# A chunked scan, a routed layer and a cosine layer in one kernel: the first expert's two token lists are cut at another tile

## The chip, the cores and the metric

The kernel runs on one core of a Trainium2 chip. The metric is the device time of one execution in microseconds (us); lower is better. TensorE (PE) multiplies matrices, VectorE (DVE), ScalarE (ACT) and GpSimd (POOL) work elementwise, and SP issues most of the DMA transfers. Each engine takes its instructions strictly in the order in which the program lists them.

## The reference, cut to what matters

```python
# 1: scan over chunks; 4 x 8 heads, 768 positions, 32 channels -> x: 3072 tokens x 256
y = (C B^T * L) x + (C state) * decay ;  state = decay_full * state + B^T x
# 2: routed layer, E = 8 experts, w1 256 x 1024, w2 1024 x 256
expert_idx = argmax(cos(x, expert_emb) / tau);  gate_w = softmax(...)[expert_idx]
for e in range(E):
    mask = expert_idx == e
    out[mask] = gate_w[mask, None] * (relu(x[mask] @ w1[e]) @ w2[e])
# 3: dense layer, w_in 256 x 2048, w_out 2048 x 256
h = x @ w_in ;  out = (h * cos(h)) @ w_out
```

## The kernel before, in words

The kernel has three stages. The first makes the tokens in 24 tiles of 128 (`for n in range(N)`, L546), finds each token's expert and sends its row into that expert's list in device memory with an indirect DMA (`scatter`, L804; one POOL instruction per tile). The tiles are routed in groups of 4, 4, 4, 4, 4, 2, 1 and 1 (`g.SIZES`, L715); a group's chain of small DVE operations (`group`, L298) hands its rows to `g.done`, from which `finish` scatters them. The second stage runs the experts one after the other (L1238). The third is the dense layer (L1354 on).

All products of the second and third stage are made from operands that are split into a rounded part and a rest (fp32r), with three matmuls for each product: high by high, rest by high, high by rest. The moving operand's width is the number of places in the list: 432 for experts 1 to 7.

Expert 0 is treated apart. Its list is cut in two. The tokens of the first twelve tiles (the groups up to number `g.EARLY = 2`) go to rows 0 to 255 of the buffer, those of the last twelve to rows 2048 to 2303. The first list is worked on by the generator `window` (L925) while the first stage is still running: a load, the gate weights (`gates`, 11 steps and one for each column of rows), transposes, 48 matmuls up, 48 down. The second list is loaded by `second_list` (L978) after the last scatter and takes expert 0's place in the loop at L1238, again with 48 and 48 matmuls.

Where a generator's next step goes in the order of the program is written out by hand: `g.WN` says how many steps of `window` stand behind tile n, and in the strings `g.TAIL` and `g.END` each letter is a step (w: `window`, x: `second_list`, c: the counts, with `fill(1)` and the load of list 1; r: `load_w1(1)`; f: `fill(2)`; k: two matmuls that only keep PE busy; g: gates of list 1; m, l, r, t in TAIL: the last tile's steps). Behind the counts stands a conditional block for lists that overflow (L1144), which every engine passes.

The SP queue behind it holds, in this order: `load_w2(1)` (L752), `rows_of(2)` (the load of list 2, L904), `fill(3)` (L891, zeros behind list 3's end), `load_w1(2)` (L746), the first pieces of the dense layer's weights (`fetch`, L1089) and `load_w2(2)`. The first of these pieces is read by ACT at L1107, in the middle of expert 1's loop.

Of the kernel before, what the change touches and what calls it, by code (L numbers as in the profile page):

```python
# [8 lines left out]
F32 = mybir.dt.float32  # L9
F32R = mybir.dt.float32r  # L10
# [3 lines left out]
AF = mybir.ActivationFunctionType  # L14
ALU = mybir.AluOpType
# [8 lines left out]
RW = 274  # L24
# [23 lines left out]
def attn_router(ctx, tc, g):  # L48

    nc = tc.nc  # L50
# [408 lines left out]
    k = 0  # L459
    while k < len(tiles):  # L460
        n = g.SIZES[len(groups)]
# [84 lines left out]
    for n in range(N):  # L546
        for k in range(max(3, n + g.AHEAD[n]), min(N, n + 1 + g.AHEAD[n + 1])):
            pre(*tiles[k])
        if n >= 3:
            logits_of(n - 3)  # L550
        t, b = tiles[n]
        if n > 1:
            front(t, b)
        if t + 1 < NSTEP:
            if b == 1:
                side = [blocks(t + 1)]
            if b == (1 if t else 3):
                preps[t + 1] = prep(t + 1)
                next(preps[t + 1])
            if b == 2 and t + 2 < NSTEP:  # L560
                load_a(t + 2)
        for s_ in side:
            next(s_, None)
            if b == 3:
                for _ in s_:
                    pass
        if n >= 1:
            t, b = tiles[n - 1]
            if n > 1:
                mid(t, b)  # L570

            if t + 1 < NSTEP:
                late.append((t + 1, b))
            while late and late[0][0] in preps:
                next(preps[late.pop(0)[0]])
            if b == 3 and t + 2 < NSTEP:
                load_b(t + 2)
        if n >= 2:
            if n == 2:
                for _ in constants_:  # L580
                    pass
            rows_of(n - 2)
        for _ in g.done[:2 if n > 12 else 1]:
            finish()
        for _ in range(g.ZN.get(n, 0)):
            next(zeros)
        g.each(n)
        win(g.WN.get(n, 0))
# [60 lines left out]


CAP = 432
CE = 256
S2 = 2048
NL = E + 1
CQ = CAP // 4
# [6 lines left out]
def tile_attention_moe_moe2(ctx: ExitStack, tc: tile.TileContext, A1, A2, X, BNh, BT, CT, cst_d, emb, tau, w1, w2, w_in, w_out, out):  # L662
    nc = tc.nc
    ET = mybir.EngineType
    g = G_()
# [10 lines left out]
    xs = dp.tile([E * SX, RW], F32, name="xs")  # L676
# [11 lines left out]
    g.FIRST = 6  # L688
    g.GE = "vava"
    g.GW = "va"  # L690
    g.EARLY = 2
    g.ZN = {4: 3, 8: 1, 13: 1}
    g.PX = 5
    g.PX0 = 4
# [32 lines left out]
    x0 = il[:, 0]  # L727
# [94 lines left out]
    def quarters(x):  # L822
        return x.rearrange("(p k) d -> p (k d)", k=4)

    def zeros(cst):

        zrow = wA.tile([CQ, 4 * RW], F32, tag="l2", name="zrow")
        nc.gpsimd.memset(zrow, 0.0)
        yield
        for k in (0, S2):  # L830
            nc.gpsimd.dma_start(quarters(xs[k:k + CE, :]), zrow[:CE // 4])
# [5 lines left out]
        nc.vector.memset(capf[:, 0:2], float(CE))  # L837
        yield
        nc.gpsimd.dma_start(quarters(zd), zrow)
        yield  # L840
# [54 lines left out]

    def places(e):

        return (CE // 2, 2) if e == 0 else (CQ, 4)

    def rows_of(e):  # L900
        P, K = places(e)
# [10 lines left out]
    def turned(xg):  # L912
        px = bank("px")
        for k in range(2):
            for m in range(2):
                nc.tensor.transpose(px.rearrange("p (m c k) -> p m c k", m=2, k=2)[:, m, :, k], xg[:, k, 136 * m:136 * m + 128], ident)
        return px

    def parts(px, xh, xl):
        nc.scalar.copy(xh, px)  # L920
        yield
        nc.vector.tensor_tensor(out=xl, in0=px, in1=xh.bitcast(F32), op=ALU.subtract)
        return [x.rearrange("p (m c) -> p m c", m=2) for x in (xh, xl)]

    def window():  # L925

        xg = xp.tile([128, 4, RW], F32, tag="xg", name="xg", bufs=2)[:, :2]
        i = nc.sync.dma_start(xg, xs[:CE, :].rearrange("(p k) d -> p k d", k=2))
        early.append(i.ins)
        yield  # L930
        yield from gates(xg, g.sb2, g.GW, -1)
        w = {k: W[0][k].rearrange("p (a b) -> p a b", a=2) for k in ("h1", "l1")}

        px = turned(xg)
        yield
        x_ = g.apool.tile([128, 1024], F32R, tag="XB0", name="x_")
        xh, xl = yield from parts(px, *(x_[:, 512 * k:512 * k + 512] for k in range(2)))
# [4 lines left out]
        hl = g.sb2.tile([128, 2048], F32R, tag="ac", name="hl")  # L942
        lo = split_lo(0, "2", g.L2)
        py = g.psY.tile([128, 2, 512], F32, tag="y", name="py")[:, :, :CE]

        def down(q):
            l2 = W[0]["l2"].rearrange("p (a b) -> p a b", a=8)
            for f in (2 * q, 2 * q + 1):
                s = slice(CE * f, CE * f + CE)
                for m in range(2):  # L950
                    for k, (a_, b_) in enumerate(((w["h2"], hh), (w["h2"], hl), (l2, hh))):
                        nc.tensor.matmul(py[:, m], lhsT=a_[:, f, 128 * m:128 * m + 128], rhs=b_[:, s], start=f == 0 and k == 0, stop=f == 7 and k == 2)
# [24 lines left out]

    def second_list():  # L978

        xg = g.xg0 = rows_of(0)  # L980
        for j in fills:
            tc.declare_no_dep(loads[0], j, reason="the first list lies before the others")
        yield
        yield from gates(xg, g.sb2, g.GW)
        yield
        px = turned(xg)
        yield
        g.x0 = yield from parts(px, *(x0[:, 512 * k:512 * k + 512] for k in range(2)))
        yield

    g.window = window()
# [58 lines left out]
    nc.scalar.copy(yd[:, :, :CE], g.y0)  # L1050
    g.pctx.close()

    with ExitStack() as mctx:
# [426 lines left out]
```

## Time and profile before

| | us |
|---|---|
| median of three runs (576.4 to 576.64) | 576.6 |
| the profiled execution, its own time | 577.55 |
| span of the profiled execution, first to last instruction | 575.9 |

The span lies 1.65 us inside the profiled execution's own time, which lies 0.95 us above the median. Times within the trace count from the start of the span. The first stage reaches to about 123 us, the experts to 297.6 us, the dense layer to the end. A matmul's bar in the trace is longer than the distance to the next one, because they overlap; the price of a matmul in a run of equal ones is that distance.

### The profile page before, as it was taken

What the parts mean: (1) busy time and instruction counts of PE and PEld (TensorE: products, weight loads), DVE (VectorE), ACT (ScalarE), POOL (GpSimd) and SP (SyncE); (2) the same over time, 40 slices, a digit from 0 to 9 for tenths busy, and PEclk for the clock granted to TensorE, in tenths of its full rate; (3) what the DMA queues carried; (4) which work ended last, traced back from release to release, by engine and by line L of the source; (5) the groups of instructions that cost most, each with busy time, mean ns of one, the idle gap of its engine ahead of it and who ended that gap; (6) DMA issues with size and microseconds to landing.
All of it is one profiled execution on the core that took longest, in us unless ns stands there. A gap on an engine that the chain in (4) does not pass through costs nothing.

```text
span 575.9 us, 10962 instructions
## 1 busy us (share of the span) xinstructions
PE 550.4 (96%) x3964; PEld 498.8 (87%) x3964; DVE 438.6 (76%) x861; ACT 294.0 (51%) x629; POOL 315.0 (55%) x348
## 2 busy tenths in 40 slices
PE   8898999989889999989999999999999999999995
PEld 4786887888879999979988999999999999999994
DVE  5997999766497798888849877766677777776882
ACT  4433444435465567656646545446445445445562
POOL 4635452452274476455636646646646745755763
PEclk9899899989989999989999999999999999999998
DMA  6999884138766655653210000000100100100000
GB/s 195 224 241 200 208 227 153 40 113 233 250 197 192 214 150 194 236 200 119 78 2 1 2 1 9 28 1 2 37 1 1 38 0 2 38 0 9 31 20 19
DMA packets 28777, 56.26 MB, mean 98 GB/s; under 512 B 7232, under 2 KB 16080, under 8 KB 28096
## 3 DMA queue, kind: packets, MB, share of 16 engines
q1 hardware_dynamic: 26032, 47.03, 28.9%
q0 software_dynamic: 2688, 8.50, 4.3%
q8 instruction: 32, 0.52, 0.4%
q14 instruction: 25, 0.20, 0.1%
HBM read 47.76 MB, written 11.07 MB: 102 GB/s over the span
## 4 chain that ended last, share of the span: by engine, by line
PE 56%; DVE 8%; issue 3%; ACT 3%; DMA 2%; POOL 1%; SPq 1%; POOLq 0%; ACTq 0%; DVEq 0%
PE po L1399 22%; PE pu L1365 22%; PE py L1224 6%; PE ph L1256 5%; DVE hl L1261 2%; DVE ta L1109 1%; POOL gl L1436 1%; DMA xg<-xs 1%; DVE ta L1111 1%; ACT hh L1260 1%; DMA r<-in_w 1%; DVE xl L1078 1%; DVE lg L861 1%; ACT h L760 1%; DVE ta L1115 1%
## 5 line engine op out<-in xcount | busy, mean ns | idle before, releaser
L1436 POOL TENSOR_TENSOR gl<-gg,gh 128x512 fp32r<-128x512 f32 (+1 forms) x111 | 125.8, 1138 | 105.1 <-PE pu L1365 63.3
L1426 ACT ACTIVATE cc<-ff,half 128x512 f32<-128x512 f32 (+1 forms) x112 | 74.2, 663 | 129.2 <-DVE ff L1424 121.6
L1422 DVE TENSOR_SCALAR tt<-pu 128x512 f32<-128x512 f32 (+1 forms) x110 | 67.4, 613 | 64.9 <-PE pu L1365 61.5
L1399 PE MATMUL po<-h,gl 128*128 128x256 f32 x384 | 108.3, 282 | 0.0
L1399 PE MATMUL po<-l,gh 128*128 128x256 f32 x384 | 108.2, 282 | 0.0
L1399 PE MATMUL po<-h,gh 128*128 128x256 f32 x382 | 107.7, 282 | 0.0
L769 POOL TENSOR_TENSOR l<-r,h 128x512 fp32r<-128x512 f32 x50 | 67.8, 1371 | 59.5 <-ACT h L760 55.7
L1399 PEld LDWEIGHTS po<-h,gh 128*128 128x128 f32 x382 | 72.3, 189 | 3.6
L1399 PEld LDWEIGHTS po<-l,gh 128*128 128x128 f32 x384 | 72.6, 189 | 3.1
L1399 PEld LDWEIGHTS po<-h,gl 128*128 128x128 f32 x384 | 73.1, 190 | 0.1
L1424 DVE SCALAR_TENSOR_TENSOR ff<-tt,pu 128x512 f32<-128x512 f32 (+1 forms) x110 | 67.0, 609 | 3.8
L1365 PE MATMUL pu<-yh,il 128*128 128x512 f32 (+1 forms) x192 | 68.6, 357 | 0.0
L1365 PE MATMUL pu<-yh,ih 128*128 128x512 f32 (+1 forms) x192 | 68.3, 356 | 0.0
L1365 PE MATMUL pu<-yl,ih 128*128 128x512 f32 (+1 forms) x192 | 68.0, 354 | 0.0
L1432 DVE SCALAR_TENSOR_TENSOR gg<-pu,cc 128x512 f32<-128x512 f32 (+1 forms) x110 | 66.6, 605 | 0.4 <-ACT cc L1426 0.4
L1435 ACT CAST gh<-gg 128x512 fp32r<-128x512 f32 (+1 forms) x112 | 60.8, 543 | 0.4 <-DVE gg L1432 0.3
L1261 DVE SCALAR_TENSOR_TENSOR hl<-ph,hh 128x432 fp32r<-128x432 f32 (+1 forms) x64 | 36.7, 576 | 23.4 <-ACT hh L1260 23.2
L1224 PE MATMUL py<-hl,h 128*128 128x432 f32 (+1 forms) x128 | 46.3, 362 | 4.1 <-DVE hl L1261 4.0
L1224 PE MATMUL py<-hh,h 128*128 128x432 f32 (+1 forms) x128 | 45.5, 356 | 1.6 <-ACT hh L1260 1.6
L1224 PE MATMUL py<-hh,l 128*128 128x432 f32 (+1 forms) x128 | 45.5, 356 | 0.0
L1260 ACT ACTIVATE hh<-ph 128x432 fp32r<-128x432 f32 (+1 forms) x64 | 32.8, 512 | 22.5 <-PE ph L1256 21.5
L1256 PE MATMUL ph<-xh,h 128*128 128x432 f32 x112 | 41.2, 368 | 0.0
(228 smaller groups left out, 1199.6 us busy)
## 6 DMA issues: line engine op xcount, KB each, us to landing
r<-in_w SPq DMA_DIRECT2D x32, 512.0 KB
ac<-acd SPq DMA_DIRECT2D x8, 512.0 KB
raw<-in_w_in SPq DMA_DIRECT2D x8, 512.0 KB
raw<-in_w_out SPq DMA_DIRECT2D x8, 512.0 KB
xg<-xs SPq DMA_DIRECT2D x7, 462.4 KB
XB<-in_X SPq DMA_DIRECT2D x10, 256.0 KB
xs<-zd SPq DMA_DIRECT2D x5, 462.4 KB
bt<-in_BT SPq DMA_DIRECT2D x6, 256.0 KB
```

The costliest lines, as they stand in the source:

```text
L769: (nc.vector if engines[q] == "v" else nc.gpsimd).tensor_tensor(out=l[:, s], in0=W[e][rn][:, s], in1=h[:, s].bitcast(F32), op=ALU.subtract)
L1224: nc.tensor.matmul(py[m][:, :b_.shape[1]], lhsT=a_[:, q, 128 * m:128 * m + 128], rhs=b_, start=q == 0 and k == 0, stop=q == 7 and k == 2)
L1256: nc.tensor.matmul(ph[:, :n], lhsT=a_[:, c, 128 * f:128 * f + 128], rhs=b_[:, c], start=k == 0, stop=k == 5)
L1261: nc.vector.scalar_tensor_tensor(out=hl, in0=ph[:, :n], scalar=0.0, in1=hh.bitcast(F32), op0=ALU.max, op1=ALU.subtract)
L1365: nc.tensor.matmul(PU[u], lhsT=a_[:, c, 128 * f:128 * f + 128], rhs=b_[:, c], start=c == 0 and k == 0, stop=c == 1 and k == 2)
L1399: nc.tensor.matmul(po[:, i], lhsT=a_[:, s], rhs=b_, start=first and per == 1, stop=q == NF - 1 and k == 2 and i == per - 1)
L1422: nc.vector.tensor_scalar(tt, pu, 0.25, MAGIC, op0=ALU.add, op1=ALU.add)
L1424: nc.vector.scalar_tensor_tensor(out=ff, in0=tt, scalar=-MAGIC, in1=pu, op0=ALU.add, op1=ALU.subtract)
L1426: nc.scalar.activation(cc, ff, AF.Sin, bias=half, scale=-TWO_PI)
L1432: nc.vector.scalar_tensor_tensor(out=gg, in0=pu, scalar=TWO_PI, in1=cc, op0=ALU.mult, op1=ALU.mult)
L1435: nc.scalar.copy(gh, gg)
L1436: (nc.vector if u >= len(units) else nc.gpsimd).tensor_tensor(out=gl, in0=gg, in1=gh.bitcast(F32), op=ALU.subtract)
```

## The change

Expert 0's lists are cut behind tile 16 instead of tile 12. The first list gets 320 places (80 partitions of four rows), the second 192 (96 partitions of two rows). Both matmul loops keep their 48 and 48 instructions; their width changes. In `window` each 128-row slice f of the hidden layer now has a PSUM bank of its own (eight evacuations of 320 columns in place of four of 512), and the transposes fill two banks. From tile 19 on up to four rows of `g.done` are scattered behind one tile. The steps of `window` begin behind tile 20 instead of 19, and TAIL and END are written anew.

```diff
-        for _ in g.done[:2 if n > 12 else 1]:
+        for _ in g.done[:4 if n > 18 else 2 if n > 12 else 1]:
             finish()
...
-CE = 256
+CE1, CE2 = 320, 192
...
-    g.EARLY = 2
+    g.EARLY = 3
...
-    g.WN = {19: 1, 20: 5, 21: 2, 22: 5}
-    g.TAIL = "tltttwtwtwmrttttttlrttttwltttttwttwttttttttttt"
-    g.END = "wxwcwccwcwwcwwwwwcwxwxwrxxfcxxxwwxxxxgxkkgkkggxxxxxg"
+    g.WN = {20: 1, 21: 7, 22: 7, 23: 1}
+    g.TAIL = "tltttwtwtmrttttttlrttttwltttttwttttwttttttttt"
+    g.END = "wxwwcwcwcwwcwwwwcwwwwwcwwwwrxxfcwxxxwwxwxxxgxkkgkkggxxxxxg"
...
-        xg = xp.tile([128, 4, RW], F32, tag="xg", name="xg", bufs=2)[:, :2]
-        i = nc.sync.dma_start(xg, xs[:CE, :].rearrange("(p k) d -> p k d", k=2))
+        xg = xp.tile([128, 4, RW], F32, tag="xg", name="xg", bufs=2)[:CE1 // 4]
+        i = nc.sync.dma_start(xg, xs[:CE1, :].rearrange("(p k) d -> p k d", k=4))
         early.append(i.ins)
         yield
-        yield from gates(xg, g.sb2, g.GW, -1)
+        yield from gates(xg, g.sb2, 2 * g.GW, -1)
...
-        for q in range(4):
-            ph = bank("ph")
-            for j in range(2):
-                f = 2 * q + j
-                k = 0
-                for c in range(2):
-                    for a_, b_ in ((w["h1"], xh), (w["h1"], xl), (w["l1"], xh)):
-                        nc.tensor.matmul(ph[:, CE * j:CE * j + CE], lhsT=a_[:, c, 128 * f:128 * f + 128], rhs=b_[:, c], start=k == 0, stop=k == 5)
-                        k += 1
-                yield
-            s = slice(512 * q, 512 * q + 512)
-            nc.scalar.activation(hh[:, s], ph, AF.Relu)
-            nc.vector.scalar_tensor_tensor(out=hl[:, s], in0=ph, scalar=0.0, in1=hh[:, s].bitcast(F32), op0=ALU.max, op1=ALU.subtract)
-            yield
-            next(lo)
-            if q >= 2:
-                down(q - 2)
-            yield
-        down(2)
-        yield
-        down(3)
-        yield
+        for f in range(8):
+            ph = bank("ph")[:, :CE1]
+            k = 0
+            for c in range(2):
+                for a_, b_ in ((w["h1"], xh), (w["h1"], xl), (w["l1"], xh)):
+                    nc.tensor.matmul(ph, lhsT=a_[:, c, 128 * f:128 * f + 128], rhs=b_[:, c], start=k == 0, stop=k == 5)
+                    k += 1
+            yield
+            hh, hl = hs[f]
+            nc.scalar.activation(hh, ph, AF.Relu)
+            nc.vector.scalar_tensor_tensor(out=hl, in0=ph, scalar=0.0, in1=hh.bitcast(F32), op0=ALU.max, op1=ALU.subtract)
+            yield
+            if f % 2 == 0:
+                next(lo)
+            if f >= 4:
+                down(f - 4)
+            yield
+        for f in range(4, 8):
+            down(f)
+            yield
...
         def wide(e):
-            return CE if e == 0 else CAP
+            return CE2 if e == 0 else CAP
```

## Rows read from the trace of the kernel before

**Rows 1.** The page: busy time and share of each engine

```profile
PE 550.4 (96%) x3964; PEld 498.8 (87%) x3964; DVE 438.6 (76%) x861; ACT 294.0 (51%) x629; POOL 315.0 (55%) x348
```

**Rows 2.** Stretches: length; busy PE, PEld, DVE, ACT, POOL; granted clock; DMA share; GB/s

```profile
115.00:120.00 5.00, 3.14 (x39) 2.80 (x38) 1.92 (x10) 1.84 (x7) 3.36 (x8) 1.00 0.32 114
120.00:125.00 5.00, 4.73 (x29) 4.56 (x30) 3.68 (x20) 2.58 (x10) 3.18 (x6) 0.69 0.18 59
...
140.00:145.00 5.00, 5.00 (x46) 5.00 (x45) 4.97 (x14) 4.72 (x12) 0.65 (x1) 1.00 0.87 226
...
155.00:160.00 5.00, 3.25 (x14) 2.51 (x14) 2.06 (x5) 3.08 (x7) 1.43 (x2) 0.95 1.05 371
```

**Rows 3.** Chain that ended last: start, length, runs of fp32r matmuls (432, 256, 512 columns)

```profile
284.62 1.18 PE ph L1256 x6
...
310.52 1.43 PE po L1399 x12
311.94 1.39 PE pu L1365 x6
```

**Rows 4.** PE in order of time: plain f32 matmuls under and at 256 columns, transposes

```profile
88.88 0.73 PE L277 MATMUL pt<-IE,yT 128*128 128x136 f32 x4
89.45 1.22 PE L214 MATMUL ps<-CB,BTb 128*128 128x256 f32 x4
...
142.03 0.91 PE L1070 MATMUL px<-ident,xg 108*128 108x108 f32 x8
```

**Rows 5.** Groups by form: PE's transposes, busy and mean ns of one

```profile
L1070 PE MATMUL px<-ident,xg 108*128 108x108 f32 x56 | 6.6, 257 | 0.6 <-DVE xg L884 0.6
```

**Rows 6.** POOL in order of time: scatters of tiles 12, 13, 16, 17, 23; list's power

```profile
100.12 1.22 POOL L805 DMA_INDIRECT xs<-yr,pi  x1 [10.26 <-ACT yr L285]
101.64 0.97 POOL L805 DMA_INDIRECT xs<-yr,pi  x1 [0.21 <-issue]
...
114.15 0.96 POOL L805 DMA_INDIRECT xs<-yr,pi  x1 [7.28 <-ACT xg L886]
115.42 0.97 POOL L805 DMA_INDIRECT xs<-yr,pi  x1 [0.23 <-ACT yT L267]
...
125.26 0.96 POOL L805 DMA_INDIRECT xs<-yr,pi  x1 [0.54 <-issue]
...
131.41 1.22 POOL L857 TENSOR_TENSOR r<-xg,pw 128x2 f32<-128x2 f32 x1 [3.62 <-DMA xg<-xs]
```

**Rows 7.** DVE in order of time: tile 22's product and group 4's sum

```profile
108.27 0.69 DVE L233 TENSOR_TENSOR M<-ps,L 128x512 f32<-128x512 f32 x1 [0.24 <-PE ps L214]
...
110.38 0.16 DVE L339 TENSOR_TENSOR acc<-acc,asum 128x8 bf16<-128x8 bf16 x1
```

**Rows 8.** PE in order of time: group 4's counts, keep-warm matmuls, expert 0's first matmuls

```profile
112.17 0.18 PE L343 MATMUL pc<-oh,tri 128*128 128x32 bf16 x1
...
134.16 1.10 PE L412 MATMUL pw<-warm 128*128 128x272 bf16 x8
...
137.00 0.50 PE L1256 MATMUL ph<-il,h 128*128 128x256 f32 x2 [1.30 <-ACTq L1144]
```

**Rows 9.** ACT in order of time: last tile, first list's result, dense layer's first weights

```profile
119.85 0.37 ACT L267 COPY yT<-py 128x256 f32<-128x256 f32 x1 [2.85 <-remote]
...
136.22 0.59 ACT L1050 COPY yd<-py 128x512 f32<-128x512 f32 x1
...
156.79 0.66 ACT L1107 ACTIVATE tb<-raw 128x512 f32<-128x512 f32 x1 [5.73 <-DMA raw<-in_w_in]
```

**Rows 10.** SP's queue in order of time: second list, `load_w2(1)`, first `fetch`

```profile
127.87 3.33 SPq L904 DMA_DIRECT2D xg<-xs  x2
...
137.72 1.90 SPq L752 DMA_DIRECT2D r<-in_w  x2
...
149.61 0.43 SPq L1089 DMA_DIRECT2D raw<-in_w_in  x1
```

**Rows 11.** Chain that ended last, around 141 us: start, length, what

```profile
141.75 6.06 DMA xg<-xs
```

More of the change, by code (lines that the diff above doesn't have):

```diff
@@ L829, in zeros @@
         yield
-        for k in (0, S2):
-            nc.gpsimd.dma_start(quarters(xs[k:k + CE, :]), zrow[:CE // 4])
+        for k, n in ((0, CE1), (S2, CE2)):
+            nc.gpsimd.dma_start(quarters(xs[k:k + n, :]), zrow[:n // 4])
             yield
@@ L836, in zeros @@
         nc.vector.memset(capf, float(CAP))
-        nc.vector.memset(capf[:, 0:2], float(CE))
+        nc.vector.memset(capf[:, 0:1], float(CE1))
+        nc.vector.memset(capf[:, 1:2], float(CE2))
         yield
@@ L896, in places @@
     def places(e):
-        return (CE // 2, 2) if e == 0 else (CQ, 4)
+        return (CE2 // 2, 2) if e == 0 else (CQ, 4)
     def rows_of(e):
@@ L910, in bank, with turned @@
         return g.psS.tile([128, 2, 4, 64], F32, tag="s", name=nm).rearrange("p a b c -> p (a b c)")
-    def turned(xg):
-        px = bank("px")
-        for k in range(2):
+    def turned(xg, wide=False):
+        P, K = xg.shape[:2]
+        px = [bank("px") for _ in range(1 + wide)]
+        px = [(px[m] if wide else px[0][:, P * K * m:])[:, :P * K] for m in range(2)]
+        for k in range(K):
             for m in range(2):
-                nc.tensor.transpose(px.rearrange("p (m c k) -> p m c k", m=2, k=2)[:, m, :, k], xg[:, k, 136 * m:136 * m + 128], ident)
+                nc.tensor.transpose(px[m].rearrange("p (c k) -> p c k", k=K)[:, :, k], xg[:, k, 136 * m:136 * m + 128], ident[:P, :P])
         return px
     def parts(px, xh, xl):
-        nc.scalar.copy(xh, px)
+        n = px[0].shape[1]
+        for m in range(2):
+            nc.scalar.copy(xh[:, m], px[m])
         yield
-        nc.vector.tensor_tensor(out=xl, in0=px, in1=xh.bitcast(F32), op=ALU.subtract)
-        return [x.rearrange("p (m c) -> p m c", m=2) for x in (xh, xl)]
+        for m in range(2):
+            nc.vector.tensor_tensor(out=xl[:, m], in0=px[m], in1=xh[:, m].bitcast(F32), op=ALU.subtract)
+        return xh, xl
     def window():
-        xg = xp.tile([128, 4, RW], F32, tag="xg", name="xg", bufs=2)[:, :2]
-        i = nc.sync.dma_start(xg, xs[:CE, :].rearrange("(p k) d -> p k d", k=2))
+        xg = xp.tile([128, 4, RW], F32, tag="xg", name="xg", bufs=2)[:CE1 // 4]
+        i = nc.sync.dma_start(xg, xs[:CE1, :].rearrange("(p k) d -> p k d", k=4))
         early.append(i.ins)
         yield
-        yield from gates(xg, g.sb2, g.GW, -1)
+        yield from gates(xg, g.sb2, 2 * g.GW, -1)
         w = {k: W[0][k].rearrange("p (a b) -> p a b", a=2) for k in ("h1", "l1")}
-        px = turned(xg)
+        px = turned(xg, True)
         yield
-        x_ = g.apool.tile([128, 1024], F32R, tag="XB0", name="x_")
-        xh, xl = yield from parts(px, *(x_[:, 512 * k:512 * k + 512] for k in range(2)))
+        x_ = g.apool.tile([128, 2048], F32R, tag="XB0", name="x_")
+        xh, xl = yield from parts(px, *(x_[:, 2 * CE1 * k:2 * CE1 * k + 2 * CE1].rearrange("p (m c) -> p m c", m=2) for k in range(2)))
         yield
@@ L942, in window @@
         hl = g.sb2.tile([128, 2048], F32R, tag="ac", name="hl")
+        he = g.sb2.tile([128, 1024], F32R, tag="BTb", name="he")
+        hs = [[z[:, CE1 * f:CE1 * f + CE1] for z in (hh, hl)] for f in range(6)]
+        hs += [[z[:, CE1 * f:CE1 * f + CE1] for z, f in ((x_, 4 + f), (he, f))] for f in range(2)]
         lo = split_lo(0, "2", g.L2)
-        py = g.psY.tile([128, 2, 512], F32, tag="y", name="py")[:, :, :CE]
-        def down(q):
+        py = g.psY.tile([128, 2, 512], F32, tag="y", name="py")[:, :, :CE1]
@@ L947, in down @@
+        def down(f):
             l2 = W[0]["l2"].rearrange("p (a b) -> p a b", a=8)
[L948 to L952, printed above, removed]
-        for q in range(4):
-            ph = bank("ph")
-            for j in range(2):
-                f = 2 * q + j
-                k = 0
-                for c in range(2):
-                    for a_, b_ in ((w["h1"], xh), (w["h1"], xl), (w["l1"], xh)):
-                        nc.tensor.matmul(ph[:, CE * j:CE * j + CE], lhsT=a_[:, c, 128 * f:128 * f + 128], rhs=b_[:, c], start=k == 0, stop=k == 5)
-                        k += 1
-                yield
-            s = slice(512 * q, 512 * q + 512)
-            nc.scalar.activation(hh[:, s], ph, AF.Relu)
-            nc.vector.scalar_tensor_tensor(out=hl[:, s], in0=ph, scalar=0.0, in1=hh[:, s].bitcast(F32), op0=ALU.max, op1=ALU.subtract)
+            hh, hl = hs[f]
+            for m in range(2):
+                for k, (a_, b_) in enumerate(((w["h2"], hh), (w["h2"], hl), (l2, hh))):
+                    nc.tensor.matmul(py[:, m], lhsT=a_[:, f, 128 * m:128 * m + 128], rhs=b_, start=f == 0 and k == 0, stop=f == 7 and k == 2)
@@ L967, in window @@
+        for f in range(8):
[5 more added lines that the diff above has]
+                    k += 1
             yield
-            next(lo)
-            if q >= 2:
-                down(q - 2)
+            hh, hl = hs[f]
+            nc.scalar.activation(hh, ph, AF.Relu)
+            nc.vector.scalar_tensor_tensor(out=hl, in0=ph, scalar=0.0, in1=hh.bitcast(F32), op0=ALU.max, op1=ALU.subtract)
@@ L987, in second_list @@
         yield
-        g.x0 = yield from parts(px, *(x0[:, 512 * k:512 * k + 512] for k in range(2)))
+        g.x0 = yield from parts(px, *(x0[:, 2 * CE2 * k:2 * CE2 * k + 2 * CE2].rearrange("p (m c) -> p m c", m=2) for k in range(2)))
         yield
@@ L1049, in tile_attention_moe_moe2 @@
     ih = yp.tile([128, 2, F2], F32R, name="ih")
-    nc.scalar.copy(yd[:, :, :CE], g.y0)
+    nc.scalar.copy(yd[:, :, :CE1], g.y0)
     g.pctx.close()
```

## The prediction

> **What bounds the kernel now.** I read the page first: PE is busy for 96% of the span [rows 1]. That would say that matmul time decides everything, and as the change keeps the number of matmuls and the sum of the two widths, that nothing happens. So I read the stretches around the change next, then each engine's order of time, then the chain of waits. In the stretches the reader is to see that PE is not full where this change works: it lacks 1.86 us of 5 in 115 to 120 and 1.75 us in 155 to 160, and in 140 to 145, in expert 0's own loop, DVE and ACT are as full as PE [rows 2].
>
> Four chains set the times there. First, PE waits in its queue for group 4's counts, which need DVE's sums; the sum ends at 110.54, PE comes at 112.17, so there is 1.6 us of room [rows 7, 8]. Second, behind the last tile all stand still: ACT's copy waits 2.85 us until 119.85 for something that the trace calls remote [rows 9]; PE idles, and in the next stretch its granted clock is 0.69, part of it at the lower level, 1.2 GHz [rows 2], which costs 5 x 0.31 = 1.5 us of full speed. Third, the second list: last scatter at 125.26, load issued at 127.87, power at 131.41 when it has landed, expert 0's first matmul at 137.00 [rows 6, 8, 10]. PE fills this with `window` until 134.16 and with 1.10 us of empty matmuls [rows 8]; the step into the loop then waits for ACT, which has just copied `window`'s result, 0.59 us at 136.22 [rows 9]. Fourth, and this decides: the transfers behind the last scatter. The load of list 2 lasts from 141.75 to 147.81 [rows 11]; SP is held behind it, so that the dense layer's first piece is issued at 149.61 [rows 10] and ACT waits 5.73 us for it, until 156.79 [rows 9]. The evacuations that PE needs stand behind that instruction in ACT's queue, and PE starves: its 1.75 us in 155 to 160. Whatever lets PE reach expert 1 earlier only makes this wait longer, unless the transfers start earlier.
>
> **Prices of matmuls.** A run of six at 432 columns takes 1.18 us, twelve at 256 take 1.43, six at 512 take 1.39 [rows 3]: 0.197, 0.119 and 0.232 us each. The line through the ends is 0.44 ns for each column, so 320 columns cost 0.147 and 192 cost 0.091 us. `window`: 96 x (0.147 - 0.119) = +2.7 us on PE. Expert 0's loop: -2.7 us. The sum is nil.
>
> No fp32r matmul under 256 columns stands in the trace, so 192 columns need bounds. From below: the line, and 0.093 us for a transpose of 108 columns, (0.91 - 0.257)/7 [rows 4, 5]. From above: plain f32 runs each product as two records (four records for the two that the code asks for), at most 0.73/4 = 0.183 us for one at 136 columns and 1.22/4 = 0.305 at 256 [rows 4]; at 192 some 0.24, twice that for a product, 0.48: the loop would take 46 us instead of 8.7. The rate of the transposes gives 0.093 x 192/108 = 0.165 us, 16 us. I take the line, as the fp32r rows are the nearest in kind and 192 is only a quarter narrower than 256; both ends stay for the range.
>
> The Trainium skill ("TensorE: Matmul & The Clock Gate", section "LDWEIGHTS (loading the stationary operand)") gives a weight load a time by its columns alone, 128/1.2 = 107 ns, which would outlast a 192-column matmul. By it the loop would take 96 x 0.107 = 10.3 us instead of 8.7, and gain 1.1 us instead of 2.7. The transposes load 128 columns each at 0.093 us [rows 4, 5], so the trace does not bear the figure out for them.
>
> **The first list is loaded late.** Before, tile 11's scatter closes it, and the load stood far ahead of its use. Now tiles 12 to 15 must land first. Their first scatter starts at 100.12, at a distance of 1.52 us [rows 6]: the fourth at 104.7, its end at 105.7. From the last scatter's end (126.22) to the issue of a load that waits for it are 1.65 us, from there to the first use 3.54 [rows 6, 10]. Estimate for the new load: issue 107.3, landed 110.8. What is queued behind it: one `gates` step on POOL (nothing else is due there until 114.15 [rows 6]), and six on DVE, right ahead of tile 22's product, which came at 108.27 [rows 7]. DVE waits there for some 3 us, and ACT's exponent behind it. Then come the power (up to 1.22 [rows 6]) and the rest of the steps, some 0.3: tile 22's product at about 112.4, group 4's sum 2.27 us later (110.54 - 108.27 [rows 7]), 114.7. PE, in order, waits for these counts from 112.2 to 114.8: +2.6 us, the 1.6 us of room used up. If the load lands 3 us sooner, this part is nothing.
>
> What of it reaches the last scatter? Below: the scatters of group 4 start about 2.0 us behind its counts (114.15 - 112.17 [rows 6, 8]), with four more column scalings between, two of them on DVE: 117.2; seven more at 1.27 us (115.42 - 114.15 [rows 6]) put the last at 126.1, +0.8. Above: the whole 2.6, if the stand-still until 119.85 comes again behind it. I take +1.5.
>
> **The window and the second list.** `window` holds PE for 2.7 us more, so the empty matmuls no longer fill a gap but stand in the way (1.10 us), and the step into the loop still needs ACT's copy of the result, now 640 columns instead of 512 (0.74 by 0.59 x 640/512). The new END places the last 6 matmuls (0.9 us) behind the second list's transposes, in a gap that PE had anyway. Second list: a quarter shorter to load, worth a few tenths at most. Sum: the loop starts at 137.0 + 2 or so, costs 2.7 us less, and PE comes to expert 1 between 1 us earlier and 1 us later. The eight evacuations in place of four cost DVE and ACT about 1 us each by their fixed parts, in a stretch (125 to 135) where both are free for some share; hidden. `load_w2(1)`, issued at 137.72 when all engines have passed the conditional block [rows 10], comes with the loop's start, up to 2 us later, and the load of list 2 stands behind it.
>
> **The sum** at the point that decides, ACT's first piece at 156.79: last scatter +1.5, later `load_w2(1)` beside list 2's load +0.5 (0 to 2), second list's shorter load nothing on this chain, PE's 2.7 us in the loop nothing, being hidden by this very wait. Together +2.0 us. Against the profiled execution's 577.55 that is 579.55; it lies 0.95 above the median of the runs, so 578.6 there. Own range of this case 577.5 to 581.
>
> **Rivals.** A measurement of this kernel tells 0.2%, 1.15 us, from nothing.
>
> *No change.* The load lands soon enough or the 1.86 us stand-still takes the delay up, the last scatter moves by less than 1 us: 576.6 (575.5 to 577.7). For it: that stand-still is as long as the delay. Against: POOL's spacing alone gives +0.8. Chance 0.2.
>
> *Faster.* The empty time of 118 to 120 does not come back, because the order has changed there; the last scatter comes 1.9 us earlier, all transfers behind it too, and then the shorter loop counts. It decides when the dense layer's first piece lands before about 155.6. 576.6 - 1.9 = 574.7. Against: DVE's late load stands ahead of it. Chance 0.12.
>
> *192 columns are too narrow for fp32r's speed.* Midway between 0.165 and 0.48 is 0.32 us: the loop takes 31 us, from 139 to about 170 instead of about 149 (137.0 + 11.4 us of matmuls + the transposes). Some 4 us of later waits go: +17, 594 (580 to 605). For it: nothing in the trace shows a narrow fp32r matmul, and every other width in the kernel is 256 or more. Against: the straight line down to 256. It decides from about 0.13 us a matmul, when the loop ends behind what ACT waits for. Chance 0.28.
>
> *The weight load binds* (the page's 107 ns). In rows: 96 x (0.107 - 0.091) = 1.6 us on a loop that ends with little room: 579.5. Chance 0.03.
>
> **How the numbers follow.** The forecast, slower by late scatters, has 0.37; it is the likeliest: 578.6. Slower 0.37 + 0.28 + 0.03 = 0.68, same 0.20, faster 0.12. Range 575.6 to 596: below it lies about half of the faster case, above it a third of the narrow one, together under 0.2.
>
> **What would show it.** Late load: DVE's first gate step of the first list with a wait for a DMA near 108 to 111, and PE waiting for group 4's counts. Last scatter: POOL's last indirect DMA behind 126. Widths: the distance of expert 0's matmuls in the loop, 0.091 us, and in `window` 0.147. Hidden gain: ACT's wait at L1107 not shorter than before. The prediction is wrong if the load lands by 108, if the last scatter is not later, or if the narrow matmuls leave the line.

## The result and the profile after

The changed kernel takes 584.63 us (median of 6 runs, 582.94 to 586.36); the kernel before, on the same chip, 576.62 (6 runs). The ratio is 1.013, with a 95% interval of 1.0107 to 1.0153: slower; the medians lie 8.0 us apart. The profiled execution of after took 583.61 us, its span is 582.0, against 575.9 before. The forecast said slower, for the right reason in its first half, and took 578.6; the range of the whole (575.6 to 596) holds the time, the forecast's own (577.5 to 581) does not. That the wide range holds it is luck: its upper end stands there for narrow matmuls in a slow mode, which did not come.

POOL in order of time, after: start, length, engine, line, what, and in brackets the idle time before it and what ended it. The first two rows shown are the first and the last of the scatters of tiles 12 to 15, which now close the first list.

```profile
98.82 1.22 POOL L805 DMA_INDIRECT xs<-yr,pi  x1 [10.33 <-ACT yr L285]
...
102.90 1.80 POOL L805 DMA_INDIRECT xs<-yr,pi  x1 [0.22 <-issue]
...
127.72 0.97 POOL L805 DMA_INDIRECT xs<-yr,pi  x1 [0.21 <-issue]
131.60 0.61 POOL L892 DMA_DIRECT2D xs<-zd  x1 [2.82 <-DVE hl L973]
...
139.19 0.56 POOL L892 DMA_DIRECT2D xs<-zd  x1 [5.19 <-DMA xg<-xs]
```

The last scatter stands at 127.72 instead of 125.26 [rows 6]: +2.46 us. This understates the change, as tile 12's scatter, which no edit touches, starts 1.30 us sooner in this execution (98.82 instead of 100.12). Counted from there the last scatter comes after 28.90 us instead of 25.14, +3.8; three more traces with the first stage of before (`e4_widths`, `e9_before_late_counts` and `e10_before_free_fills` below) have 24.89 to 25.88, three more with the changed one (`e2_counts_early`, `e6_second_256` and `e11_after_free_fills`) 28.85 to 29.34. Behind it `fill(1)` (the first row L892) waits 2.82 us, by the trace for a product of DVE that belongs to `window`; before it stood at 127.19, now at 131.60: +4.41. DVE in order of time shows both causes:

```profile
109.61 0.19 DVE L862 TENSOR_TENSOR lg<-xg 80x32 f32<-80x32 f32 x1 [3.82 <-DMA xg<-xs]
...
111.34 0.68 DVE L233 TENSOR_TENSOR M<-ps,L 128x512 f32<-128x512 f32 x1
...
122.45 0.17 DVE L356 TENSOR_TENSOR po<-pc,oh 128x16 f32<-128x16 f32 x1 [1.97 <-remote]
...
129.41 0.49 DVE L973 SCALAR_TENSOR_TENSOR hl<-ph,hh 128x320 fp32r<-128x320 f32 x1 [0.85 <-ACT hh L972]
129.89 0.15 DVE L1015 TENSOR_TENSOR endi<-cnt,base 1x9 int32<-1x9 f32 x1
```

The first gate step waits 3.82 us for the late load, and tile 22's product behind it comes at 111.34 instead of 108.27 [rows 7]. At the other end `endi`, which `fill(1)` needs, stands behind an evacuation of `window` (L973), which waits for ACT and so for PE. Before, the steps of the counts ran in one piece up to it, and `fill(1)` followed 1.72 us behind its start (127.19 - 125.47), as it does now (131.60 - 129.89 = 1.71). DVE and POOL before:

```profile
125.47 0.15 DVE L1008 TENSOR_TENSOR endi<-cnt,base 1x9 int32<-1x9 f32 x1
...
127.19 0.60 POOL L891 DMA_DIRECT2D xs<-zd  x1 [0.87 <-issue]
```

So it is `endi` that sets `fill(1)`, and not the last scatter. PE after, in order of time, and the stretches (length; busy PE, PEld, DVE, ACT, POOL; granted clock; DMA share; GB/s):

```profile
113.13 0.18 PE L343 MATMUL pc<-oh,tri 128*128 128x32 bf16 x1 [1.89 <-DVE oh L329]
...
122.77 0.73 PE L277 MATMUL pt<-IE,yT 128*128 128x136 f32 x4 [2.27 <-ACT yT L267]
...
125.34 0.90 PE L968 MATMUL ph<-x__1730,h 128*128 128x320 f32 x2
...
130.83 0.47 PE L968 MATMUL ph<-x__1730,l 128*128 128x320 f32 x1
131.10 0.50 PE L968 MATMUL ph<-x__1730,h 128*128 128x320 f32 x2
...
140.39 1.10 PE L412 MATMUL pw<-warm 128*128 128x272 bf16 x8
...
143.70 0.47 PE L1263 MATMUL ph<-il,h 128*128 128x192 f32 x2 [0.97 <-ACTq L1151]
...
144.34 0.27 PE L1263 MATMUL ph<-il,l 128*128 128x192 f32 x1
144.45 0.39 PE L1263 MATMUL ph<-il,h 128*128 128x192 f32 x2
144.68 0.27 PE L1263 MATMUL ph<-il,l 128*128 128x192 f32 x1
```
```profile
115.00:120.00 5.00, 5.00 (x60) 4.73 (x57) 2.86 (x13) 2.04 (x8) 3.05 (x5) 0.75 0.16 58
120.00:125.00 5.00, 2.16 (x19) 1.85 (x18) 2.54 (x18) 2.47 (x10) 2.46 (x7) 0.94 0.16 56
125.00:130.00 5.00, 4.95 (x20) 4.88 (x21) 2.80 (x12) 0.88 (x2) 3.35 (x6) 0.50 0.34 117
130.00:135.00 5.00, 5.00 (x32) 5.00 (x32) 3.00 (x10) 1.31 (x3) 1.62 (x2) 0.88 0.40 137
```

PE waits 1.89 us for group 4's counts, where it waited for nothing before [rows 8]. The stand-still behind the last tile comes again, 2.27 us long, and after it the clock is granted at 0.50, 1.2 GHz, through the whole stretch 125 to 130 (0.96 there before): 21 matmuls of `window` from 125.34 to 131.10 stand 0.274 us apart instead of 0.147. The wait for group 4's counts has such a stretch behind it too: 0.75 in 115 to 120, where before had 1.00 [rows 2], and from group 4's counts to group 5's (113.13 to 120.33) PE needs 7.20 us instead of 5.81 (112.17 to 117.98). Expert 0's 192-column matmuls stand 0.111 us apart. The rest of the chain is in SP's queue and on ACT, after:

```profile
130.37 4.94 SPq L905 DMA_DIRECT2D xg<-xs  x2
136.89 0.83 SPq L746 DMA_DIRECT2D r<-in_w  x2
139.98 0.36 SPq L850 DMA_DIRECT2D dense<-few  x1
142.04 1.15 SPq L752 DMA_DIRECT2D r<-in_w  x2
145.47 0.36 SPq L905 DMA_DIRECT2D xg<-xs  x1
152.19 0.66 SPq L892 DMA_DIRECT2D xs<-zd  x1
```
```profile
162.00 0.66 ACT L1114 ACTIVATE tb<-raw 128x512 f32<-128x512 f32 x1 [4.71 <-DMA raw<-in_w_in]
```

ACT's first piece of the dense layer comes at 162.00 instead of 156.79 [rows 9], +5.2, and the first matmul of the dense layer at 302.62 instead of 297.43, again +5.2. Expert 1's first matmul is later by more: 155.38 instead of 149.16, +6.2. From ACT's first piece to the dense layer are 140.6 us in both, so the end moves with that piece. There are two late paths to it, PE's own work and the transfers, and the experiments have to say which one costs the time.

### The profile page after: what moved, and what is told of

Its sections match the earlier page's. It is cut to its first block, busy times and chain, and to the rows that moved or that the text cites. A ratio compares the mean times of both kernels' runs of the same rounds, so it can differ in the third digit from the quotient of the medians.

```text
span 582.0 us, 10988 instructions
## 1 busy us (share of the span) xinstructions
PE 555.6 (95%) x3968; PEld 501.4 (86%) x3968; DVE 439.4 (76%) x869; ACT 295.7 (51%) x636; POOL 315.3 (54%) x348
## 4 chain that ended last, share of the span: by engine, by line
PE 52%; DVE 11%; issue 3%; ACT 3%; POOL 2%; DMA 1%; POOLq 0%; DVEq 0%; ACTq 0%; SPq 0%
PE po L1406 22%; PE pu L1372 20%; PE py L1231 5%; PE ph L1263 4%; DVE hl L1268 3%; POOL gl L1443 1%; DVE ta L1116 1%; DVE ta L1118 1%; DVE il L1126 1%; DVE xg L885 1%; DVE xl L1085 1%; DMA pidf<-dense 1%; DVE ta L1122 1%; DVE lg L862 1%; ACT hh L1267 1%
## 5 line engine op out<-in xcount | busy, mean ns | idle before, releaser
L1372 PEld LDWEIGHTS pu<-yl,ih 128*128 128x128 f32 x192 | 36.2, 188 | 5.6
```

The lines of the kernel that those rows point to most:

```text
L1372: nc.tensor.matmul(PU[u], lhsT=a_[:, c, 128 * f:128 * f + 128], rhs=b_[:, c], start=c == 0 and k == 0, stop=c == 1 and k == 2)
```

## The experiments

Twelve kernels ran; each ratio is against runs of the kernel before on the same chip. The first stage's times move between single executions of the same code: tile 12's scatter starts at 97.45 to 100.12 in four traces that share before's first stage, at 98.50 to 98.93 in four that share the changed one. Places in two traces are to be read with that margin.

**The late load.** `e1_gates_later` puts `window`'s seven steps from behind tile 21 behind tile 22, and the next seven from there behind tile 23.

```diff
-    g.WN = {20: 1, 21: 7, 22: 7, 23: 1}
+    g.WN = {20: 1, 22: 7, 23: 8}
```

> The changed kernel with the first list's six first gate steps one tile later (behind tile 22 instead of 21), so that the load has landed when VectorE asks for it. Theory A (the late load delays the last tiles): VectorE's wait for the load, 3.8 us in the changed kernel, falls under 0.5 us; the last scatter comes 1.5 to 2.5 us earlier than its 127.7; the time falls by 2 to 3 us from 584.6. Theory B (the transfers behind the last scatter are late because the counts stand behind the window's evacuations) and theory C (the narrow matmuls cost too much): within 1 us of 584.6.

584.37 us, ratio 1.0096 (1.006 to 1.0131). The wait for the load shrinks to 0.48 us, and PE reaches group 4's counts at 112.14 without a wait; the last scatter comes at 126.22, 1.5 us sooner, though this execution's load was issued 1.35 us later. The loop starts 1.2 us sooner (142.52), but ACT's first piece comes at 162.65, no sooner: something else holds the end. The edit changed more than the wait for the load. The stand-still behind the last tile shrank to 0.39 us, while PE now waits 1.37 us for ACT's scaling of list 1, and its clock is granted at 0.53 on the mean from 119 to 130. That the late load delays the last scatter fits, but this run does not single it out; and its interval, some 2 us either way, would not show a gain of 1 us.

**The place of the counts.** `e2_counts_early` moves the counts and `fill(1)` to the head of END.

```diff
-    g.END = "wxwwcwcwcwwcwwwwcwwwwwcwwwwrxxfcwxxxwwxwxxxgxkkgkkggxxxxxg"
+    g.END = "wxcccwwwwwwcwwwwcwwwwwcwwwwrxxfcwxxxwwxwxxxgxkkgkkggxxxxxg"
```

> The changed kernel with the counts' first three steps placed in one piece ahead of the second evacuation of the window, everything else in its order. All theories: the zeros behind list 1 start about 2 us earlier than 131.6. Theory B: the transfers behind them and the dense layer's first weights come 2 us earlier and the time falls by 2 us. Theory A: TensorE reaches expert 0's second list no earlier (143.7, bound by the window's matmuls), and the time falls by 0.7 us at most.

583.85 us, ratio 1.0103 (1.0067 to 1.0139). `fill(1)` moves to 129.23 (-2.4) and `load_w2(1)` to 140.94 (-1.1), while the loop starts at 143.85, no sooner. So `load_w2(1)` does not wait for the loop's start, as the prediction had it. List 2's load is issued 1.0 us sooner (144.46), yet `fill(3)` behind it only at 152.82: this load took 1.6 us longer than after's, and ACT's first piece gains 0.6.

**The new order without the new cut.** `e3_old_cut` is the changed kernel with 256 and 256 places and the cut behind tile 12.

```diff
-CE1, CE2 = 320, 192
+CE1, CE2 = 256, 256
...
-    g.EARLY = 3
+    g.EARLY = 2
```

> The changed kernel with the cut behind tile 12 again and 256 and 256 places, but with its new order of steps, its eight evacuations and its scatters of up to four behind one tile. Theory A: the load is early again, the window is 2.7 us shorter, 577 to 578.5 us. Theory B: the order alone costs, 580 us or more. Theory C: 577 or less, as the matmuls are 256 wide.

581.47 us, ratio 1.0043 (1.0019 to 1.0067). The new order, with its eight evacuations, costs 0.4% by itself, some 2.5 us of the 8; cut and widths cost the rest. `fill(1)` stands at 129.86 here too, 3.2 us behind the last scatter (126.66) where before it was 1.9.

**The price of narrow matmuls.** `e4_widths` is the kernel before; its matmuls of the second list run over 256, 240, 224, 192, 160, 128, 96 and 64 columns, one width for each f.

```diff
+                if e == 0:
+                    n = (256, 240, 224, 192, 160, 128, 96, 64)[f]
...
-                        nc.tensor.matmul(ph[:, :n], lhsT=a_[:, c, 128 * f:128 * f + 128], rhs=b_[:, c], start=k == 0, stop=k == 5)
+                        nc.tensor.matmul(ph[:, :n], lhsT=a_[:, c, 128 * f:128 * f + 128], rhs=b_[:, c, :n], start=k == 0, stop=k == 5)
```

> The kernel before, in which the eight hidden slices of expert 0's second list are multiplied at 256, 240, 224, 192, 160, 128, 96 and 64 columns (most of that list's result is left out): the price of one fp32r matmul by its width. By the straight line of the prediction: 0.119, 0.112, 0.105, 0.091, 0.077, 0.063, 0.048, 0.034 us. By a floor, as the changed kernel's 0.111 us at 192 columns suggests: 0.119, 0.112 and then 0.111 us at all narrower widths. A step to several times more under some width is what the prediction's rival had. Time of the whole within 1 us of 576.6 in each case.

One run, 576.4 us. PE in order of time, matmuls of 256, 192 and 64 columns:

```profile
137.52 0.28 PE L1224 MATMUL py<-hh,h 128*128 128x256 f32 x1
137.64 0.28 PE L1224 MATMUL py<-hl,h 128*128 128x256 f32 x1
...
142.31 0.27 PE L1224 MATMUL py<-hh,h 128*128 128x192 f32 x1
142.42 0.27 PE L1224 MATMUL py<-hl,h 128*128 128x192 f32 x1
...
142.81 0.28 PE L1258 MATMUL ph<-il,l 128*128 128x64 f32 x1
142.92 0.39 PE L1258 MATMUL ph<-il,h 128*128 128x64 f32 x2
143.14 0.28 PE L1258 MATMUL ph<-il,l 128*128 128x64 f32 x1
```

The distance is 0.12 us at 256 columns, 0.11 at 192, and at 64 still 0.11 ((143.14 - 142.92)/2). From 240 columns down it is flat: the straight line of the prediction ends there, and no slow mode comes in its place. The narrow rival falls.

**The widths in the changed kernel.** `e5_first_272` has 272 places in the first list, `e6_second_256` has 256 in the second.

```diff
-CE1, CE2 = 320, 192
+CE1, CE2 = 272, 192
```
```diff
-CE1, CE2 = 320, 192
+CE1, CE2 = 320, 256
```

> The changed kernel with 272 places for the first list in place of 320 (it holds 271 tokens, so nothing is lost); 192 for the second. Theory 1, PE's way through the window sets the time of the transfers behind it: 272 columns cost about 0.126 us between the 0.119 of 256 and the 0.147 of 320, 96 x 0.021 = 2.0 us less on PE and some tenths more at half clock; the empty matmuls move from 140.4 to about 138.2, expert 0's loop from 143.7 to about 141.5, ACT's first piece from 162.0 to about 160, the whole about 2 us under the changed kernel, ratio to before about 1.009. Theory 2, the last scatter and the second list set it: POOL's fill(1) stays, ACT's first piece stays at 162, the whole is that of the changed kernel, ratio 1.013.

586.73 us, ratio 1.0141 (1.0077 to 1.0205). Neither theory is met. From the last tile's transposes to the empty matmuls are 15.0 us (125.21 to 140.22) where after needs 17.6, 2.6 less; how much of it is the width is not shown, as the clock was also low for a shorter time (0.91 in 130 to 135, and 0.74 instead of 0.50 in 125 to 130). But the first list's load landed 2.5 us later (DVE waits 6.08 us for it, until 112.13), the last scatter stood at 130.10, and the gain was gone. Whether the load's length comes from its 68 partitions was not tried.

> The changed kernel with 256 places for the second list in place of 192; the first keeps 320. Theory 1, the loop's width is hidden by ACT's wait for the dense layer's first piece: the loop's 96 matmuls go from 0.111 back to 0.119 us, 0.8 us more on PE, and the whole moves by less than 0.5 us, ratio to before 1.012 to 1.014. Theory 2, the second list's shorter load and loop are on the path: a quarter more rows to load and 0.8 us more of loop give 1 us or more, ratio 1.015.

584.22 us, ratio 1.0113 (1.0058 to 1.0168): not to be told from after. The interval is some 3 us either way, so that 0.8 us of loop could not be seen in it: that the width is hidden is neither shown nor refuted.

**The idle time and the clock.** `e7_filled_stall` is the changed kernel, `e8_before_filled_stall` the kernel before, with 16 empty matmuls where PE stands still.

```diff
+        if gi == 5:
+            pk = g.psS.tile([128, 2, 4, 64], F32, tag="s", name="pk").rearrange("p a b c -> p (a b c)")
+            for _ in range(16):
+                nc.tensor.matmul(pk[:, :272], lhsT=warm[:, :128], rhs=warm[:, :272], start=True, stop=True)
```

> The changed kernel with 16 empty matmuls of 272 columns behind the counts of group 5, in front of the last tile's transposes: that is where PE stands idle from 120.5 to 122.8 and where the clock falls afterwards. Theory 1, only the signal to ACT and DVE is late and the low clock comes from the idle time: the empty matmuls start at 120.5, end by 122.8, nothing is later, the granted clock of 125 to 130 goes from 0.50 to near 1.00, the window's matmuls come 2.5 to 2.9 us sooner, ACT's first piece about 2 us sooner; ratio to before about 1.009. Theory 2, PE itself stands still (its instructions are late): the empty matmuls start only near 122.4, the last tile's transposes come 2 us later, the last scatter 1.5 to 2 us later; ratio about 1.015. Theory 3, the clock does not depend on this idle time: PE row as in theory 1, the clock stays low, ratio 1.013.

PE in order of time, then the stretch (columns as above), then ACT, in `e7_filled_stall`:

```profile
120.14 0.17 PE L346 MATMUL pc<-oh,onesb 128*128 128x8 bf16 x1
120.16 2.01 PE L353 MATMUL pk<-warm 128*128 128x272 bf16 x16
122.73 0.73 PE L277 MATMUL pt<-IE,yT 128*128 128x136 f32 x4 [0.56 <-ACT yT L267]
```
```profile
125.00:130.00 5.00, 4.81 (x32) 4.46 (x33) 4.02 (x15) 1.72 (x4) 3.29 (x6) 1.00 0.32 114
```
```profile
163.42 0.67 ACT L1118 ACTIVATE tb<-raw 128x512 f32<-128x512 f32 x1 [4.17 <-DMA raw<-in_w_in]
```

The empty matmuls run at once, and the clock is then granted in full where it was 0.50. From the last tile's transposes to the empty matmuls in front of the loop PE needs 15.47 us instead of 17.62: the low clock cost it 2.15. The idle time alone does not settle the clock, though: in `e9_before_late_counts` and `e10_before_free_fills` PE stands still for 2.28 and 2.31 us in the same place, and the clock stays at 1.00. The last tile's transposes are not later. The loop starts 1.7 us sooner (142.00). But list 2's load is issued at 146.69 and ACT's first piece comes at 163.42; the time, 584.48 us, ratio 1.0114 (1.0061 to 1.0167), can't be told from after's. A gain on PE of 1.7 us vanished in the wait for transfers.

> The kernel before with the same 16 empty matmuls behind group 5's counts. Theory 1: half clock from 121.9 to 125.2 goes, which is 1.6 us on PE, of which up to 1.5 reach ACT's first piece; ratio to before 0.997 to 0.9995. Theory 2: the last tile's transposes come 2 us later, ratio 1.002 to 1.004. Theory 3: 1.000.

577.8 us, ratio 0.9991 (0.9958 to 1.0023). The low clock is gone here too (1.00 in 120 to 125 where [rows 2] has 0.69), and the time stays within its interval of 2 us either way: ACT waits 6.14 us for the first piece. On PE itself half clock costs next to nothing in the kernel before: from the last tile's transposes to the empty matmuls are 13.89 us there, and 13.74 here and in `e10_before_free_fills`, at full clock.

**The transfers.** `e9_before_late_counts` is the kernel before with the counts four steps of `window` later.

```diff
-    g.END = "wxwcwccwcwwcwwwwwcwxwxwrxxfcxxxwwxxxxgxkkgkkggxxxxxg"
+    g.END = "wxwwwwwwccccwcwwwcwxwxwrxxfcxxxwwxxxxgxkkgkkggxxxxxg"
```

> The kernel before, cut and sizes untouched; only END is changed, so that the counts and with them fill(1) stand four window steps later, as the new END has them behind evacuations of the window. Theory 1, the chain fill(1), load of list 1, fill(2), load of list 2, fill(3), first piece of the dense layer sets the time: fill(1) goes from 127.2 to 129 or 130, ACT's first piece from 156.8 to 159 or 160, ratio 1.003 to 1.006. Theory 2, PE's way through the window and expert 0's loop sets it: PE's rows stay, ratio 1.000.

580.47 us, ratio 1.0063 (1.004 to 1.0087). `fill(1)` comes at 129.84, 6.0 us behind the last scatter instead of 1.9, and the first piece at 159.84. PE's rows did not stay, though: its loop waits 2.35 us for DVE's `il` at 138.54. The order of the counts alone can cost 3 us and more, but this run does not separate the two paths.

The next three do. `fill(3)` stands in SP's queue behind list 2's load and waits until it has landed; `fill(2)` waits so for list 1's. The zeros behind one list's end and another list's rows lie in different blocks of 4096 rows, so that the wait protects nothing. `e10_before_free_fills` and `e11_after_free_fills` free all fills of it, in the kernel before and in the changed one.

```diff
-        if e == 0:
-            loads.append(i.ins)
+        loads.append(i.ins)
```

> The kernel before; the zeros behind one list's end no longer wait for the load of another list (they lie 4096 rows apart). Theory 1 (the chain of fills and loads): fill(2) follows without waiting for list 1's load, fill(3) at 142 to 143 instead of 147.8, the first fetch at 144 instead of 149.6, ACT's wait of 5.73 us shrinks to under 2, PE's wait of 1.57 us in front of expert 1's first down matmul and the half clock behind it go; 2 to 3 us faster, ratio 0.994 to 0.997. Theory 2 (PE bound): ratio 0.999 to 1.000. Theory 3 (contention): the transfers start earlier and land no earlier; 1.000.

572.68 us, ratio 0.9921 (0.9894 to 0.9949): 4.6 us faster than before, more than expected. SP and ACT in `e10_before_free_fills`:

```profile
137.40 0.37 SPq L904 DMA_DIRECT2D xg<-xs  x1
139.06 0.65 SPq L891 DMA_DIRECT2D xs<-zd  x1
143.18 0.85 SPq L746 DMA_DIRECT2D r<-in_w  x2
144.07 0.91 SPq L1088 DMA_DIRECT2D raw<-in_w_in  x2
```
```profile
151.96 0.66 ACT L1106 ACTIVATE tb<-raw 128x512 f32<-128x512 f32 x1 [2.35 <-DMA raw<-in_w_in]
```

`fill(3)` follows list 2's load after 1.7 us instead of some 6.1 [rows 11]. The first piece is read 4.8 us sooner, of which 1.6 belong to this execution's earlier last scatter (123.64); the wait of 1.57 us that PE had before, in expert 1's matmuls down, is gone. From the first piece to the dense layer are 140.6 us as before, so the gain lies in front of that piece and not in the later fills, which the edit frees too. So it was the transfers that held the kernel before here.

> The changed kernel with the same freed fills. Theory 1: ACT's wait of 4.71 us for the first piece shrinks to under 2, PE's wait of 0.57 us goes; PE then comes as its own work lets it, expert 1 at 155.4, some 6 us behind before: 1 to 2 us faster than the changed kernel, ratio to before 1.009 to 1.012, and 5 us or more slower than e10_before_free_fills. Theory 2, only the transfers were late and PE's lateness is not felt: ratio near that of e10_before_free_fills.

581.46 us, ratio 1.0082 (1.005 to 1.0115); SP, ACT and PE in `e11_after_free_fills`:

```profile
144.79 0.66 SPq L892 DMA_DIRECT2D xs<-zd  x1
151.65 0.84 SPq L746 DMA_DIRECT2D r<-in_w  x2
152.53 1.67 SPq L1095 DMA_DIRECT2D raw<-in_w_in  x2
```
```profile
159.62 0.66 ACT L1113 ACTIVATE tb<-raw 128x512 f32<-128x512 f32 x1 [1.92 <-DMA raw<-in_w_in]
```
```profile
155.80 0.38 PE L1262 MATMUL ph<-xh,h 128*128 128x432 f32 x1
```

PE no longer waits for ACT in expert 1, and the kernel is still 8.8 us behind `e10_before_free_fills` on the same chip (581.46 - 572.68). With `fill(3)` out of the way, PE's lateness is felt almost in full (7.7 us at the first piece, 8.1 at expert 1), and the rows show how: `load_w1(2)` (L746), which stands in front of the first pieces in SP's queue, waits 6.3 us for DVE's evacuations of expert 0's loop (3.6 in `e10_before_free_fills`), and these wait for PE. Against after, the freed fills let it start only 1.3 us sooner (151.65 instead of 152.96) before it met that wait: so near to each other are the two paths there.

`e12_after_mended` joins four edits of the changed kernel: freed fills, the gate steps of `e1_gates_later` (`g.WN` as there), the 16 empty matmuls, and the counts early.

```diff
-    g.END = "wxwwcwcwcwwcwwwwcwwwwwcwwwwrxxfcwxxxwwxwxxxgxkkgkkggxxxxxg"
+    g.END = "wxwcccwwwwwcwwwwcwwwwwcwwwwrxxfcwxxxwwxwxxxgxkkgkkggxxxxxg"
```

> The changed kernel with four edits: freed fills, the window's gate steps behind tile 22 instead of 21, counts at the head of END, and 16 empty matmuls in the idle time behind group 5's counts. If the parts found are all there is (late load, late counts, half clock, transfers behind them), the last scatter comes at 126.2, fill(1) at 128, expert 0's loop near 140, expert 1 near 151.5 against 149.2 before, and the time is 1 to 2 us above before and 3 to 4 above e10_before_free_fills: ratio to before 1.000 to 1.004. If something else in the cut costs time, it stays above 1.006.

577.68 us, ratio 1.0013 (0.9989 to 1.0038). The places of five traces, in us from the start of each span:

| | before | after | e10 | e11 | e12 |
|---|---|---|---|---|---|
| last scatter (POOL) | 125.26 | 127.72 | 123.64 | 128.27 | 125.84 |
| `fill(1)` (POOL) | 127.19 | 131.60 | 125.49 | 132.16 | 128.60 |
| load of list 2 (SP) | 141.75 | 145.47 | 137.40 | 143.15 | 139.74 |
| `fill(3)` (SP) | 147.83 | 152.19 | 139.06 | 144.79 | 141.19 |
| first piece (ACT) | 156.79 | 162.00 | 151.96 | 159.62 | 156.72 |
| expert 0's loop (PE) | 137.00 | 143.70 | 135.56 | 144.12 | 140.49 |
| expert 1's first matmul (PE) | 149.16 | 155.38 | 147.72 | 155.80 | 152.58 |
| dense layer's first matmul (PE) | 297.43 | 302.62 | 292.56 | 300.23 | 296.21 |

Beside the freed fills, the mends take 3.8 us off (581.46 - 577.68), and 5.0 us remain to `e10_before_free_fills` (577.68 - 572.68), more than the 3 to 4 expected. In the two traces expert 1 starts 4.9 us later (152.58 instead of 147.72): 2.8 up to the last tile's transposes (121.81 instead of 118.98), 1.6 from there to the empty matmuls, which is the wider window, and 0.5 in the step into the loop. PE in `e12_after_mended`:

```profile
119.09 2.89 PE L353 MATMUL pk<-warm 128*128 128x272 bf16 x16
121.81 0.63 PE L277 MATMUL pt<-IE,yT 128*128 128x136 f32 x4
```

Here one of the mends is itself in the way. The stand-still that the 16 empty matmuls were to fill does not come: ACT's copy starts at 119.17, 0.11 us behind PE's last matmul, and ends at 119.54, yet the transposes that need it start at 121.81, behind the empty matmuls. Some 2.2 us of the 4.9 may be theirs; what they save by the clock was not separated. So the 5.0 us are not the price of the cut alone. In no version here did the cut pay; the best is the kernel before with freed fills.

## Why the prediction was right and where it was wrong

*The late load: right.* Predicted issue at 107.3, landing at 110.8, DVE waiting some 3 us, PE waiting for group 4's counts until 114.8. Measured: issue 106.25, first use 109.61, a wait of 3.82 us, PE's counts at 113.13. The earlier scatter start (98.82 instead of the 100.12 that I worked with) accounts for 1.3 us of the difference.

*The last scatter: right in kind, taken too small.* +2.46 us, or +3.8 counted from tile 12's scatter, against +1.5 taken and +2.6 as upper end. The condition named there held: the stand-still did come again behind it (2.27 us). What the bound lacked is the clock behind the wait for the load: 7.20 us instead of 5.81 from group 4's counts to group 5's. That the late load is the cause is argued from the order of these rows; `e1_gates_later` brings the scatter 1.5 us forward, but changes the stand-still as well.

*Prices: one right, one wrong.* 320 columns cost 0.147 us as worked out. 192 columns cost 0.111, not 0.091: the line was drawn past its end, and by the prediction's own third sign of being wrong, narrow matmuls that leave the line, it was wrong here. The loop saved (0.119 - 0.111) x 96 = 0.8 us, not 2.7. The Trainium skill ("TensorE: Matmul & The Clock Gate", section "LDWEIGHTS (loading the stationary operand)") gives a weight load 107 ns for 128 columns, by a formula in which the moving width does not appear. The flat distance of `e4_widths`, 0.111 us, is within 4% of that figure. That rival, given 0.03, was right about the price; that it is the weight load which sets the distance no run shows by itself, and what 0.8 us more of loop would do to the whole, `e6_second_256` cannot tell.

*The failed step: "The window and the second list".* It had expert 0's loop start at 137.0 + 2 and PE come to expert 1 within 1 us of before. Measured: 143.70 and +6.2. The parts are on PE: the last tile's transposes come 2.5 later (122.77 instead of 120.27); from there to the empty matmuls 17.62 us instead of 13.89, of which 2.0 is half clock (17.62 - 15.47 in `e7_filled_stall`, against 13.89 - 13.74 in `e8_before_filled_stall`) and 1.7 the width of the 90 matmuls that stand there (15.47 - 13.74), the last six following the empty ones; the step into the loop 3.31 instead of 2.84; and from the loop's start to expert 1, 11.68 instead of 12.16. Sum 2.5 + 3.7 + 0.5 - 0.5 = 6.2. I had carried the late scatter into the transfers, and not into PE's own path, where the same stand-still delays the window as well; I had set the loop's saving against the window's cost; and I had read half clock from its share of a stretch (1.5 us in the kernel before, where PE lost 0.15) and had no term for it behind the wider window, where it cost 2.15.

*The end point: right place, wrong size.* ACT's first piece does decide before (`e10_before_free_fills`), but it came +5.2 later, not +2.0. The term that I had at +0.5, `load_w2(1)`, hangs on another chain than I thought: `fill(1)`, list 1's load, POOL's `few`, SP's L850, then `load_w2(1)`. I read the new END for PE's order and not for DVE's, where `endi` moved behind `window`'s evacuations: 4.41 of the 5.2 us are there at `fill(1)` already. Of these, 2.2 come with PE's last count matmul (125.24 instead of 123.05), and 2.2 more between it and `endi` (4.65 us instead of 2.42); in `e7_filled_stall`, where the clock stays full, this distance is 3.14, so that 1.5 belong to the clock and 0.7 to the order. `e2_counts_early` bears the chain out in part, as 2.4 us at `fill(1)` became 1.1 at `load_w2(1)`; behind it the gain was lost in a longer load.

*"Hidden by ACT's wait": right before, half right after.* In the changed kernel PE's lateness and that of the transfers are nearly level. Mending one alone moved nothing that could be told apart (`e1_gates_later`, `e2_counts_early`, `e7_filled_stall`); freeing the fills alone left 1.0082, and the other mends on top of them 1.0013. The freed fills speed up the kernel before as well, by 4.6 us, so that 1.0013 does not mean that the cut became free. The profile's 6.1 us in span divide into 5.2 up to the dense layer and 0.9 in it. The medians lie 8.0 apart, because the profiled execution of before was 0.9 us slower than its median and that of after 1.0 faster; 1.3 of this stands already at tile 12's scatter.

## What to carry to other kernels

When an order written by hand is changed, read it once for every engine: a small instruction that a transfer waits for may have moved behind a large one that waits for something else. A stall found at the head of a stage delays every path that leaves it, so add it to each of them before setting gains against costs. And where two late paths are level, an experiment on one shows nothing; free one of them in both kernels, and compare again. A mend that fills idle time has to be looked at once more when other edits have moved that idle time: in `e12_after_mended` it had gone, and the filling delayed what stood behind it.

## What the runs showed of the hardware that was not expected

An fp32r matmul against a 128 x 128 weight does not come closer than 0.11 us to the next, from 240 columns down to 64 (`e4_widths`); narrower lists save nothing there.

After 2.27 us of idle PE, and 1.5 us of matmuls at their full rate, the clock was at 1.2 GHz for 5.8 us of dense matmuls (125.34 to 131.10); with the idle time filled by 2.01 us of empty matmuls it was 1.00 from 120 to 135 (`e7_filled_stall`). It does not fall behind every such gap: after 2.28 and 2.31 us in the same place it stayed at 1.00 (`e9_before_late_counts`, `e10_before_free_fills`). What decides between the two is open.

The stand-still itself stays unexplained: ACT and DVE get their signal some 2 us behind PE's last matmul in front of it, before and after alike. In `e1_gates_later` and `e12_after_mended`, where the gate steps stand one tile later, ACT has it after 0.13 and 0.11 us, so that it hangs on the order of the steps in some way that no run shows; and `e7_filled_stall` shows that PE itself is not held, since its next 16 matmuls run at once.
